# Moving a conversion piece's integer operations ahead of the weights' low parts in every odd slot of a retention, experts and feed-forward kernel

## The chip, the cores and the metric

The kernel runs on one core of a Trainium2 chip. The metric is the time of one execution in device microseconds; three runs of the kernel before took 1249.22, 1249.59 and 1250.06 us, with a median of 1249.59 us.

## The reference

Three stages follow each other, all in float32. First a retention layer (2 x 8 heads, 768 positions, 64 columns), whose output has 1536 rows of 512 columns. Then a layer of 8 experts, whose gate is normalised by eight rounds of row and column sums. Then a feed-forward layer with `h - tanh(h)`.

```python
def _moe_ref(x, w_gate, w1, w2):
    ...
    for _ in range(8):
        P /= P.sum(1, keepdims=True) + 1e-09
        P /= P.sum(0, keepdims=True) + 1e-09
        P *= N / E
    for e in range(E):
        h = np.maximum(x @ w1[e], 0.0)
        out += P[:, e:e + 1] * (h @ w2[e])

def _moe2_ref(x, w_in, w_out):
    h = x @ w_in
    return ((h - np.tanh(h)) @ w_out)
```

The weights of the last layer, `moe2_w_in` and `moe2_w_out`, arrive as 64-bit floats, two 32-bit words each, and the kernel itself turns them into float32.

## The kernel before

Every float32 operand of a product is split into a high part (`...h`, a copy rounded by ACT) and a low part (`...l`, the difference, made by DVE or POOL), and every product is three matmuls: high by high, low by high, high by low. `split` (L174) makes such a pair. Products of `x` and the first weights follow a Strassen scheme with seven products per block (`product`, L807; `xp...` are plain blocks of `x`, `xs...` sums of blocks).

The middle of the program is a loop over 64 **slots** (L835), each the work of one quarter of an expert's weights on one half of the rows. A slot has a fixed order on PE: products 1, 2, 5 and 6; the second matmuls (`tiles`, L617, result bank `yq`) of the slot before for its tiles 0 to 2; product 7; tiles 3 to 5; products 4 and 3. The banks of `yq` are three in turn, so tile 3 uses the bank of tile 0. DVE adds each `yq` to `yacc` (L641). Between the products ACT copies partial sums to SBUF (`sa`, `sb`) and DVE adds them to other banks (`pbl` L859, `pah` L871, `pbh` L882). ACT reads `sb` from the bank of `pal` before product 7 goes on adding to it. The hidden layer's high and low parts are `h0h`, `h0l`, `h1h`, `h1l` (`relu`, L677); DVE's second `h1l` of a slot frees the bank that the next slot's `pbh` writes.

Odd slots bring in the next weights. `w_load` (L117) loads them to `wraw`, which has one buffer; `w1_split` and `w2_split` make `w1h`, `w1l`, `w2h`, `w2l`. DVE makes two low parts of `w1l`, POOL the other four and those of `w2l`. The new `wraw` can be loaded when POOL has made the last `w2l`.

Beside this, from slot 5 to slot 60, the last layer's weights are converted in 64 **pieces** (`conv`, L563), one in most slots and two in ten even slots. A piece has steps: step 0 issues the load of the words `d` on SP's queue; step 1 is five integer operations on DVE (L580 to L587, on buffers `c0` and `c1`), then two on POOL (L588, L589); step 2 is two more on DVE (L591, L592), which wait for POOL; steps 3 to 5 split the result, or sums of results, into blocks `hl` (`block`, L553; five buffers in turn) and store them to DRAM (`wscr`). A store is not issued where its block is made: it is put on a list, and `flush` (L540) issues what stands there. At a step 1 all of the list is issued; at other steps only what came from earlier slots.

What is done at which point of a slot stands in four lists, `fd`, `fa`, `fb` and `fc`, filled from L733 on by `put` and emptied once in each slot: `fd` behind product 5, `fa` behind product 7, `fb` behind tile 5, `fc` at the slot's end. Each engine runs its instructions in the order in which they are written, and SP issues its DMAs in that order.

```python
flush(j == 1)
...
box[q, p].append(cq.tile([128, NC64], I32, tag=f"c1_{count[0] % 7}", name=f"c1_{u}_{i}"))
...
for steps in (((fa, s - 1), (fa, s), (fc, s)), ((fd, s), (fb, s), (fd, s + 1)))[:1 + more]:
```

The last line gives the places of steps 0, 1 and 2 of a slot's first and second piece.

Of the kernel before, what the change touches and what calls it, by code (L numbers as in the profile page):

```python
# [11 lines left out]
I32 = mybir.dt.int32  # L12
# [9 lines left out]
NCH = N // CH  # L22
# [14 lines left out]
NS = len(SLOTS)  # L37
NC64 = 256
# [17 lines left out]
def kernel(  # L56
# [27 lines left out]
    def bank(name):  # L84
        return psh.tile([128, 512], F32, tag="h", name=name)
# [118 lines left out]
    attn = ctx.enter_context(ExitStack())  # L204
# [331 lines left out]
    box = {}  # L536

    stores, now, count = [], [0], [0, 0, 0]

    def flush(all=False):  # L540
        while stores and (all or stores[0][0] < now[0]):
            stores.pop(0)[2]()
# [10 lines left out]
    def block(q, o, src, pair=False):  # L553
        tag = f"hl{count[1] % 5}"
        t = staged(tag, 256, f"hl{q}_{o}")
        count[1] += 1
        if pair:
            split(halves(t[:, 0]), halves(t[:, 1]), odds(src), nc.gpsimd)
        else:
            split(t[:, 0], t[:, 1], src, nc.gpsimd)  # L560
        store(q, o, t, tag)

    def conv(u, i, j):  # L563
        q, p = 2 * u + i // 8, i % 8
        flush(j == 1)
        if j == 0:
            d = cq.tile([128, NC64, 2], I32, tag=f"d{count[2] % 3}", name=f"d{u}_{i}")
            count[2] += 1
            nc.sync.dma_start(out=d.rearrange("p n t -> p (n t)"),
                              in_=wio[u].bitcast(I32)[:, i * 2 * NC64:(i + 1) * 2 * NC64])  # L570
            c0 = cp.tile([128, NC64], I32, tag="c0", name=f"c0_{u}_{i}")
            box[q, p] = [d, c0]
            return
        if j == 1:
            box[q, p].append(cq.tile([128, NC64], I32, tag=f"c1_{count[0] % 7}", name=f"c1_{u}_{i}"))
            count[0] += 1
        d, c0, c1 = box[q, p]
        hi, lo, val = d[:, :, 1], d[:, :, 0], c1.bitcast(F32)
        if j == 1:
            nc.vector.tensor_scalar(out=c0, in0=hi, scalar1=3, scalar2=0x40000000,  # L580
                                    op0=ALU.logical_shift_left, op1=ALU.bitwise_xor)
            nc.vector.tensor_scalar(out=c1, in0=hi, scalar1=-0x80000000, scalar2=None, op0=ALU.bitwise_and)
            nc.vector.scalar_tensor_tensor(out=c0, in0=c0, scalar=0x7FFFFFFF, in1=c1,
                                           op0=ALU.bitwise_and, op1=ALU.bitwise_or)
            nc.vector.tensor_scalar(out=val, in0=lo.bitcast(U32), scalar1=2.0 ** -52,
                                    scalar2=None, op0=ALU.mult)
            nc.vector.tensor_scalar(out=lo, in0=c0, scalar1=-0x800000, scalar2=None, op0=ALU.bitwise_and)  # L587
            nc.gpsimd.tensor_tensor(out=val, in0=val, in1=lo.bitcast(F32), op=ALU.mult)  # L588
            nc.gpsimd.tensor_tensor(out=val, in0=val, in1=c0.bitcast(F32), op=ALU.add)  # L589
        elif j == 2:  # L590
            nc.vector.tensor_scalar(out=lo, in0=hi, scalar1=0x7FFFFFFF, scalar2=None, op0=ALU.bitwise_and)  # L591
            nc.vector.scalar_tensor_tensor(out=val, in0=lo.bitcast(F32), scalar=thr, in1=val,  # L592
                                           op0=ALU.is_ge, op1=ALU.mult)
        elif j == 3:
            if p < 3:
                block(q, (0, 256, 1536)[p], val)
            elif p == 3:
                a11, a22 = (box[q, k][2].bitcast(F32) for k in (0, 2))
                nc.gpsimd.tensor_tensor(out=a22, in0=val, in1=a22, op=ALU.add)
                nc.gpsimd.tensor_tensor(out=val, in0=a11, in1=val, op=ALU.subtract)  # L600
            else:
                block(q, 1792 + 256 * (p - 4), val, True)
        elif j == 4:
            a11, a12, a22 = (box[q, k][2].bitcast(F32) for k in range(3))
            block(q, WI[5], a22)
            block(q, WI[7], val)
            nc.gpsimd.tensor_tensor(out=a11, in0=a22, in1=a11, op=ALU.subtract)
            nc.gpsimd.tensor_tensor(out=a12, in0=a12, in1=a11, op=ALU.subtract)
        else:
            a11, a12 = (box[q, k][2].bitcast(F32) for k in range(2))  # L610
            block(q, WI[6], a11)
            block(q, WI[3], a12)
# [117 lines left out]
        if X2[n][1]:  # L730
            x2_sum(b, X2[n][1], eng)

    spots = [{s: [] for s in range(NS)} for _ in range(4)]  # L733
    fd, fa, fb, fc = spots

    def put(f, s, what, *a):
        f[s].append(lambda: what(*a))

    for q in range(2, NQE):
        s = 2 * q - 1  # L740
# [35 lines left out]
    put(fa, 1, stage, 0)  # L776
    put(fa, 1, sblocks, NCH - 2)
    put(fb, 1, w2_split, 1, 0)
    put(fb, 1, raws, NCH - 3)
    put(fb, 1, raws, NCH - 2)  # L780
    for what, a in ((sblocks, (NCH - 1,)), (w2_split, (1, 1)), (raws, (NCH - 1,))):
        put(fc, 1, what, *a)
    for j in range(1, NST):
        put((fa, fc)[(j - 1) % 2], 2 + (j - 1) // 2, stage, j)
    for c in range(NCH):
# [3 lines left out]
    n = 0  # L789
    for s in range(lo_, hi_):  # L790
        more = s % 2 == 0 and (s - lo_) // 2 * extra // ((hi_ - lo_) // 2) != ((s - lo_) // 2 + 1) * extra // ((hi_ - lo_) // 2)
        for steps in (((fa, s - 1), (fa, s), (fc, s)), ((fd, s), (fb, s), (fd, s + 1)))[:1 + more]:
            for j, (f, at_) in enumerate(steps):
                put(f, at_, conv, n // (nconv // NQ), n % (nconv // NQ), j)
            f, at_ = (fd, at_ + 1) if f is fc else (fb, at_)
            for j in (3, 4, 5) if n % 8 == 3 else (3,):
                put(f, at_ + j - 3, conv, n // (nconv // NQ), n % (nconv // NQ), j)
            n += 1
# [31 lines left out]
    def run(fs):  # L830
        for f in fs:
            f()

    pend = None
    for s in range(NS):  # L835
        if s == 1:
            yp_, sm = (ctx.enter_context(tc.tile_pool(name=n, bufs=1, reuse_waits="tile")) for n in ("yp", "sm"))
        now[0] = s
        if s == 2:
            attn.close()  # L840
            attn = ctx.enter_context(ExitStack())
            cp = attn.enter_context(tc.tile_pool(name="cp", bufs=2, side="right", reuse_waits="tile"))
            cq = attn.enter_context(tc.tile_pool(name="cq", bufs=1, side="right", reuse_waits="tile"))
        if s == NS - 2:
            flush(True)
# [13 lines left out]
        nc.vector.tensor_tensor(out=pbl, in0=pbl, in1=sa, op=ALU.add)  # L859
        product(pbh, s, 5, True)  # L860
        nc.scalar.activation(out=sa, in_=pbh, func=ACTF.Copy)
        run(fd[s])
        product(pal, s, 6, False)
        nc.scalar.activation(out=sb, in_=pal, func=ACTF.Copy)
# [94 lines left out]
    for g in range(ng):  # L959
        f = [bank(f"f{i}_{g}") for i in range(2)]  # L960
# [122 lines left out]
```

## Time and profile before

| what | value |
|---|---|
| median of three runs | 1249.59 us |
| the profiled execution's own time | 1250.11 us |
| its span, first to last instruction | 1248.3 us |
| PE busy | 1233.6 us, 99% |
| DVE busy | 995.8 us, 80% |
| ACT busy | 589.8 us, 47% |
| POOL busy | 536.9 us, 43% |
| granted clock of TensorE | 1.000 over the span |

The own time is the span and 1.8 us around it. Busy shares are averages over the whole program, which has three stages. Times in the views are counted from the start of the span. Matmuls overlap: a row of 512 columns lasts 0.38 us, but the next starts 0.22 us later.

### The profile page before, as it was taken

Reading aid. Unit: us, or ns where it says so; the run is one execution under the profiler, and the core shown is the slowest. Engines: PE = TensorE matmul, PEld = TensorE weight load, DVE = VectorE, ACT = ScalarE, POOL = GpSimd, SP = SyncE. Lnnn points to the kernel's source line nnn. Section 1 sums busy time; section 2 is a strip of 40 time slices with the busy share of each in tenths; the row PEclk is TensorE's granted clock in tenths of the full one; section 3 lists DMA queues with packets and bytes.
Section 4 is the critical chain, followed back from the end, with each engine's and each line's share of the span. In section 5 each row is a group of like instructions: output and inputs, shape, how many; then the busy total and the mean of one; then the engine's idle time right before and its main releaser. Section 6 shows DMA issues by size and latency. Waiting matters only on the chain. (4 is left out here: it accounts for less than half of the span.)

```text
span 1248.3 us, 20284 instructions
## 1 busy us (share of the span) xinstructions
PE 1233.6 (99%) x7450; PEld 1138.0 (91%) x7450; DVE 995.8 (80%) x1914; ACT 589.8 (47%) x1191; POOL 536.9 (43%) x696
## 2 busy tenths in 40 slices
PE   8999999999999999999999999999999999999998
PEld 6899999999999999999999999999999889999997
DVE  6978888877778787787787878778785788888987
ACT  4653333433333433333333443333333388888875
POOL 4853444644645555554554654554462022131000
PEclk9999999999999999999999999999999999999999
DMA  9311122322322332322232232222334266384571
GB/s 327 132 34 43 43 68 68 112 83 68 110 68 78 103 111 81 110 76 77 76 93 77 88 98 77 85 85 77 94 95 182 93 233 232 110 279 143 199 266 68
DMA packets 63635, 141.84 MB, mean 114 GB/s; under 512 B 6064, under 2 KB 33200, under 8 KB 63536
## 3 DMA queue, kind: packets, MB, share of 16 engines
q1 hardware_dynamic: 63104, 140.02, 33.7%
q8 instruction: 58, 0.95, 0.3%
q10 hardware_dynamic: 432, 0.53, 0.1%
q14 instruction: 41, 0.34, 0.1%
HBM read 114.32 MB, written 26.21 MB: 113 GB/s over the span
## 5 line engine op out<-in xcount | busy, mean ns | idle before, releaser
L641 DVE SCALAR_TENSOR_TENSOR yacc<-yq,prob,yacc 128x512 f32<-128x512 f32 x336 | 240.1, 745 | 105.5 <-PE yq L628 104.9
L178 POOL TENSOR_TENSOR hl<-c,hl 128x256 fp32r<-128x256 f32 x88 | 71.1, 819 | 190.7 <-ACT hl L176 190.7
L626 PE MATMUL yq<-w2h,h1h 128*128 128x512 f32 x384 | 146.3, 381 | 0.0
L628 PE MATMUL yq<-w2h,h1l 128*128 128x512 f32 x384 | 145.6, 379 | 0.0
L627 PE MATMUL yq<-w2l,h1h 128*128 128x512 f32 x384 | 145.6, 379 | 0.0
L626 PE MATMUL yq<-w2h,h0h 128*128 128x512 f32 x384 | 145.5, 379 | 0.0
L627 PE MATMUL yq<-w2l,h0h 128*128 128x512 f32 x384 | 145.5, 379 | 0.0
L628 PE MATMUL yq<-w2h,h0l 128*128 128x512 f32 x384 | 145.5, 379 | 0.0
L813 PE MATMUL pal<-xsh,w1h 128*128 128x384 f32 x384 | 125.6, 327 | 0.0
L815 PE MATMUL pal<-xsl,w1h 128*128 128x384 f32 x384 | 125.2, 326 | 0.0
L816 PE MATMUL pal<-xsh,w1l 128*128 128x384 f32 x384 | 125.2, 326 | 0.0
L679 ACT ACTIVATE h1h<-pah 128x384 fp32r<-128x384 f32 x64 | 31.4, 491 | 177.5 <-PE yq L627 171.9
L588 POOL TENSOR_TENSOR c<-c,d 128x256 f32<-128x256 f32 x64 | 47.5, 742 | 138.5 <-DVE d L587 134.1
L178 POOL TENSOR_TENSOR w1l<-wsum,w1h 128x256 fp32r<-128x256 f32 x124 | 91.1, 765 | 31.5 <-ACT w1h L176 31.5
L178 POOL TENSOR_TENSOR w2l<-wraw,w2h 128x512 fp32r<-128x512 f32 x64 | 83.8, 1330 | 6.4 <-ACT w2h L176 6.4
L679 ACT ACTIVATE h0h<-pbl 128x384 fp32r<-128x384 f32 x64 | 31.7, 496 | 110.4 <-PE yq L627 110.4
L628 PEld LDWEIGHTS yq<-w2h,h1l 128*128 128x128 f32 x384 | 72.6, 189 | 10.7 <-DVE h1l L680 0.4
L627 PEld LDWEIGHTS yq<-w2l,h0h 128*128 128x128 f32 x384 | 72.6, 189 | 10.3
L628 PEld LDWEIGHTS yq<-w2h,h0l 128*128 128x128 f32 x384 | 72.6, 189 | 10.3
L626 PEld LDWEIGHTS yq<-w2h,h0h 128*128 128x128 f32 x384 | 72.6, 189 | 10.3
L626 PEld LDWEIGHTS yq<-w2h,h1h 128*128 128x128 f32 x384 | 72.6, 189 | 7.6 <-DVE yacc L641 0.5
L627 PEld LDWEIGHTS yq<-w2l,h1h 128*128 128x128 f32 x384 | 72.6, 189 | 7.1 <-POOL w2l L178 0.3
(228 smaller groups left out, 3599.0 us busy)
## 6 DMA issues: line engine op xcount, KB each, us to landing
wraw<-in_w SPq DMA_DIRECT2D x64, 512.0 KB, 4.8
wscr<-hl SPq DMA_DIRECT2D x88, 256.0 KB, 2.6
d<-in_wio SPq DMA_DIRECT2D x64, 256.0 KB, 3.3
w1h<-wscr SPq DMA_DIRECT2D x18, 768.0 KB, 4.5
w1l<-wscr SPq DMA_DIRECT2D x18, 768.0 KB, 5.9
w2h<-wscr SPq DMA_DIRECT2D x18, 512.0 KB, 3.8
w2l<-wscr SPq DMA_DIRECT2D x18, 512.0 KB, 4.7
qk<-in_qkv SPq DMA_DIRECT2D x11, 512.0 KB, 8.6
```

Of the source, the lines that this page charges most:

```text
L178: eng.tensor_tensor(out=lo, in0=src, in1=hi.bitcast(F32), op=ALU.subtract)
L588: nc.gpsimd.tensor_tensor(out=val, in0=val, in1=lo.bitcast(F32), op=ALU.mult)
L626: nc.tensor.matmul(out=yp, lhsT=hi, rhs=pairs(w2h[q][:, i]), start=i == 1, stop=False)
L627: nc.tensor.matmul(out=yp, lhsT=hi, rhs=pairs(w2l[q][:, i]), start=False, stop=False)
L628: nc.tensor.matmul(out=yp, lhsT=lo, rhs=pairs(w2h[q][:, i]), start=False, stop=i == 0)
L641: nc.vector.scalar_tensor_tensor(out=y, in0=yp, scalar=prob[:, c, q // 4:q // 4 + 1], in1=y, op0=ALU.mult, op1=ALU.add)
L679: nc.scalar.activation(out=hi, in_=ps, func=ACTF.Relu)
L813: nc.tensor.matmul(out=ps, lhsT=w1h[q][:, ws], rhs=pairs(xh[:, k]), start=start and k == 0, stop=False, skip_group_check=True)
L815: nc.tensor.matmul(out=ps, lhsT=w1h[q][:, ws], rhs=pairs(xl[:, k]), start=False, stop=False, skip_group_check=True)
L816: nc.tensor.matmul(out=ps, lhsT=w1l[q][:, ws], rhs=pairs(xh[:, k]), start=False, stop=k == 1, skip_group_check=True)
```

## The change

In odd slots step 1 of a piece moves from `fa`, behind product 7, to a new list `fe`, which is emptied right ahead of `fd`. Step 1 is also where `flush` issues the whole list of stores. `c0` is now taken at step 1 and has one buffer instead of two, and `c1` has eight instead of seven. In the start of the loop the split of the rows of chunks 9, 10 and 11 (`raws`) moves from slot 1 to `fd` of slot 2, the last blocks of sums (`sblocks`) come earlier within slot 1, and the pools of the first stage are closed one slot later.

```diff
-            c0 = cp.tile([128, NC64], I32, tag="c0", name=f"c0_{u}_{i}")
-            box[q, p] = [d, c0]
+            box[q, p] = [d]
             return
         if j == 1:
-            box[q, p].append(cq.tile([128, NC64], I32, tag=f"c1_{count[0] % 7}", name=f"c1_{u}_{i}"))
+            box[q, p].append(cp.tile([128, NC64], I32, tag="c0", name=f"c0_{u}_{i}"))
+            box[q, p].append(cq.tile([128, NC64], I32, tag=f"c1_{count[0] % 8}", name=f"c1_{u}_{i}"))
...
-    put(fb, 1, raws, NCH - 3)
-    put(fb, 1, raws, NCH - 2)
-    for what, a in ((sblocks, (NCH - 1,)), (w2_split, (1, 1)), (raws, (NCH - 1,))):
-        put(fc, 1, what, *a)
+    put(fb, 1, sblocks, NCH - 1)
+    put(fc, 1, w2_split, 1, 1)
+    for c in range(NCH - 3, NCH):
+        put(fd, 2, raws, c)
...
-        for steps in (((fa, s - 1), (fa, s), (fc, s)), ((fd, s), (fb, s), (fd, s + 1)))[:1 + more]:
+        for steps in (((fa, s - 1), ((fa, fe)[s % 2], s), (fc, s)), ((fd, s), (fb, s), (fd, s + 1)))[:1 + more]:
...
-        if s == 2:
+        if s == 3:
...
-            cp = attn.enter_context(tc.tile_pool(name="cp", bufs=2, side="right", reuse_waits="tile"))
+            cp = attn.enter_context(tc.tile_pool(name="cp", bufs=1, side="right", reuse_waits="tile"))
...
         nc.scalar.activation(out=sa, in_=pbh, func=ACTF.Copy)
+        run(fe[s])
         run(fd[s])
```

DVE in slot 23, before, from the addition to `pbl` to the first use of `h0l` (the number in a name is the slot, the piece or the load):

```order
L859 TENSOR_TENSOR pbl23_4249<-pbl23_4249,sa_896 128x384
L178 TENSOR_TENSOR w1l12_4275<-wraw12_4102,w1h12_4274 128x512
L178 TENSOR_TENSOR w1l12_4275<-wraw12_4102,w1h12_4274 128x256
L591 TENSOR_SCALAR d1_3_4136<-d1_3_4136 128x256
L592 SCALAR_TENSOR_TENSOR c1_1_3_4221<-d1_3_4136,c1_1_3_4221 128x256
L641 SCALAR_TENSOR_TENSOR yacc0_1065<-yq22_0_4292,prob_76,yacc0_1065 128x512
L641 SCALAR_TENSOR_TENSOR yacc0_1065<-yq22_1_4300,prob_76,yacc0_1065 128x512
L641 SCALAR_TENSOR_TENSOR yacc0_1065<-yq22_2_4308,prob_76,yacc0_1065 128x512
L871 TENSOR_TENSOR pah23_4322<-pal23_4248,sa_896 128x384
L580 TENSOR_SCALAR c0_1_4_4194<-d1_4_4192 128x256
```

The same place in the change:

```order
L859 TENSOR_TENSOR pbl23_4248<-pbl23_4248,sa_896 128x384
L580 TENSOR_SCALAR c0_1_4_4273<-d1_4_4191 128x256
L582 TENSOR_SCALAR c1_1_4_4274<-d1_4_4191 128x256
L583 SCALAR_TENSOR_TENSOR c0_1_4_4273<-c0_1_4_4273,c1_1_4_4274 128x256
L585 TENSOR_SCALAR c1_1_4_4274<-d1_4_4191 128x256
L587 TENSOR_SCALAR d1_4_4191<-c0_1_4_4273 128x256
L178 TENSOR_TENSOR w1l12_4283<-wraw12_4100,w1h12_4282 128x512
L178 TENSOR_TENSOR w1l12_4283<-wraw12_4100,w1h12_4282 128x256
L591 TENSOR_SCALAR d1_3_4135<-d1_3_4135 128x256
L592 SCALAR_TENSOR_TENSOR c1_1_3_4220<-d1_3_4135,c1_1_3_4220 128x256
L641 SCALAR_TENSOR_TENSOR yacc0_1065<-yq22_0_4300,prob_76,yacc0_1065 128x512
```

The five integer operations stood behind `pah` and now stand between `pbl` and the low parts; L591 and L592 belong to the second piece of slot 22. On POOL the two operations L588 and L589 move with them, ahead of the slot's `hl` and `w1l` parts.

SP's queue around slots 11 and 12, before (`wraw7` is the load at the end of slot 11; `hl0_512` to `hl0_2048` are made in slot 11, the three after them in slot 12):

```order
L551 DMA wscr0_77<-hl0_512_2562 256x1x256
L551 DMA wscr0_77<-hl0_1024_2565 256x1x256
L551 DMA wscr0_77<-hl0_1792_2570 256x1x256
L569 DMA d0_7_2630<-in_wio 128x512
L121 DMA wraw7_2685<-in_w12 128x1024 x2
L551 DMA wscr0_77<-hl0_2048_2665 256x1x256
L551 DMA wscr0_77<-hl0_768_2717 256x1x256
L551 DMA wscr0_77<-hl0_1280_2720 256x1x256
L551 DMA wscr0_77<-hl0_2304_2723 256x1x256
```

The same place in the change:

```order
L569 DMA d0_7_2627<-in_wio 128x512
L121 DMA wraw7_2681<-in_w12 128x1024 x2
L551 DMA wscr0_77<-hl0_512_2570 256x1x256
L551 DMA wscr0_77<-hl0_1024_2573 256x1x256
L551 DMA wscr0_77<-hl0_1792_2578 256x1x256
L551 DMA wscr0_77<-hl0_2048_2661 256x1x256
L551 DMA wscr0_77<-hl0_768_2716 256x1x256
L551 DMA wscr0_77<-hl0_1280_2719 256x1x256
L551 DMA wscr0_77<-hl0_2304_2722 256x1x256
```

Three stores that stood ahead of the loads of `d` and `wraw` now stand behind them. The blocks take the five `hl` buffers in turn in the order in which they are made: `hl0_1280` has the buffer of `hl0_512`, and `hl0_2304` that of `hl0_1024`.

DVE at the end of slot 1, the piece of the difference (`-` before, `+` the change, rows without a sign in both):

```order
-L178 TENSOR_TENSOR xpl_1_97<-xr_803,xph_1_94 128x4x64
-L178 TENSOR_TENSOR xpl_1_97<-xr_847,xph_1_94 128x4x64
-L680 SCALAR_TENSOR_TENSOR h1l<-pah_1089,h1h 128x384
-L680 SCALAR_TENSOR_TENSOR h1l<-pal_1015,h1h 128x384
-L882 TENSOR_TENSOR pbh_1017<-pbh_1017,sb 128x384
 L178 TENSOR_TENSOR xsl_1_95<-xr_744,xsh_1_92 128x8x64
 L178 TENSOR_TENSOR xsl_1_95<-ts_1046,xsh_1_92 128x4x64
 L178 TENSOR_TENSOR xsl_1_96<-ts_1046,xsh_1_93 128x4x64
+L680 SCALAR_TENSOR_TENSOR h1l<-pah_1089,h1h 128x384
+L680 SCALAR_TENSOR_TENSOR h1l<-pal_1015,h1h 128x384
+L883 TENSOR_TENSOR pbh_1017<-pbh_1017,sb 128x384
+L680 SCALAR_TENSOR_TENSOR h0l<-pbh_1017,h0h 128x384
```

The two `xpl` parts of chunks 9 and 10 leave slot 1, and the three `xsl` parts stand ahead of the two `h1l` instead of behind them. In slot 2 the three `xpl` parts of chunks 9 to 11 follow the addition to `pbl`.

## Rows read from the trace of the kernel before

**Rows 1.** The page: busy time of each engine, and two of the costliest groups.
```profile
PE 1233.6 (99%) x7450; PEld 1138.0 (91%) x7450; DVE 995.8 (80%) x1914; ACT 589.8 (47%) x1191; POOL 536.9 (43%) x696
...
L641 DVE SCALAR_TENSOR_TENSOR yacc<-yq,prob,yacc 128x512 f32<-128x512 f32 x336 | 240.1, 745 | 105.5 <-PE yq L628 104.9
...
L588 POOL TENSOR_TENSOR c<-c,d 128x256 f32<-128x256 f32 x64 | 47.5, 742 | 138.5 <-DVE d L587 134.1
```

**Rows 2.** Waits: engine, line, who was waited for, us in total, times, longest.
```profile
PEld yq L626 <- DVE yacc L641: 0.5, 2, 0.3
```

**Rows 3.** Timeline of PE at the end of slot 11: start, us, engine, line, operation.
```profile
229.54 0.43 PE L813 MATMUL pbh<-xsh,w1h 128*128 128x384 f32 x1 [0.43 <-DVE h1l L680]
```

**Rows 4.** Timeline of PE early in slot 2.
```profile
80.86 0.43 PE L815 MATMUL pbh<-xsl,w1h 128*128 128x384 f32 x1 [0.25 <-DVE xsl L178]
```

**Rows 5.** Timeline of DVE in slot 23.
```profile
393.55 1.03 DVE L178 TENSOR_TENSOR w1l<-wraw,w1h 128x512 fp32r<-128x512 f32 x2 [1.16 <-ACT w1h L176]
394.50 0.91 DVE L591 TENSOR_SCALAR d<-d 128x256 int32<-128x256 int32 x1
395.51 0.49 DVE L592 SCALAR_TENSOR_TENSOR c<-d,c 128x256 f32<-128x256 f32 x1
395.92 2.03 DVE L641 SCALAR_TENSOR_TENSOR yacc<-yq,prob,yacc 128x512 f32<-128x512 f32 x3
```

**Rows 6.** Timeline of PE in slot 23, first product of tile 3.
```profile
397.00 0.38 PE L626 MATMUL yq<-w2h,h1h 128*128 128x512 f32 x1
```

**Rows 7.** Timeline of all engines in slot 55.
```profile
863.94 2.03 DVE L641 SCALAR_TENSOR_TENSOR yacc<-yq,prob,yacc 128x512 f32<-128x512 f32 x3
...
865.01 0.38 PE L626 MATMUL yq<-w2h,h1h 128*128 128x512 f32 x1
```

**Rows 8.** Timeline of all engines in slot 17.
```profile
306.92 0.33 DVE L591 TENSOR_SCALAR d<-d 128x256 int32<-128x256 int32 x1
...
307.76 2.06 DVE L641 SCALAR_TENSOR_TENSOR yacc<-yq,prob,yacc 128x512 f32<-128x512 f32 x3
...
309.43 0.38 PE L626 MATMUL yq<-w2h,h1h 128*128 128x512 f32 x1
```

**Rows 9.** Timeline of DVE in slot 16, first and next after one piece's integer operations.
```profile
295.58 0.32 DVE L580 TENSOR_SCALAR c<-d 128x256 int32<-128x256 int32 x1
...
297.22 0.54 DVE L680 SCALAR_TENSOR_TENSOR h0l<-pbl,h0h 128x384 fp32r<-128x384 f32 x1
```

**Rows 10.** Timeline of POOL in slot 11.
```profile
226.25 0.75 POOL L588 TENSOR_TENSOR c<-c,d 128x256 f32<-128x256 f32 x1 [0.64 <-DVE d L587]
...
227.76 2.56 POOL L178 TENSOR_TENSOR w2l<-wraw,w2h 128x512 fp32r<-128x512 f32 x2
```

**Rows 11.** Timeline of SP's queue, slots 11 and 12.
```profile
230.35 0.81 SPq L121 DMA_DIRECT2D wraw<-in_w  x2
231.26 4.73 SPq L551 DMA_DIRECT2D wscr<-hl  x4
```

**Rows 12.** DMA issues from 231.1 to 231.9 us: KB each, us to landing.
```profile
wraw<-in_w SPq DMA_DIRECT2D x1, 512.0 KB, 5.4
wscr<-hl SPq DMA_DIRECT2D x1, 256.0 KB, 5.6
```

**Rows 13.** Timeline of all engines in slot 12.
```profile
233.86 0.48 ACT L864 ACTIVATE sb<-pal 128x384 f32<-128x384 f32 x1
...
235.48 0.33 PE L813 MATMUL pal<-xsh,w1h 128*128 128x384 f32 x1
```

**Rows 14.** Timeline of all engines in slot 32.
```profile
522.59 0.43 SPq L569 DMA_DIRECT2D d<-in_wio  x1
...
524.24 1.15 ACT L176 ACTIVATE hl<-c 128x256 fp32r<-128x256 f32 x3
...
527.38 0.33 PE L813 MATMUL pal<-xsh,w1h 128*128 128x384 f32 x1
```

**Rows 15.** DMA issues from 522.5 to 523 us: KB each, us to landing.
```profile
d<-in_wio SPq DMA_DIRECT2D x1, 256.0 KB, 5.0
```

More of the change, by code (lines that the diff above doesn't have):

```diff
@@ L731, in x2_step @@
             x2_sum(b, X2[n][1], eng)
-    spots = [{s: [] for s in range(NS)} for _ in range(4)]
-    fd, fa, fb, fc = spots
+    spots = [{s: [] for s in range(NS)} for _ in range(5)]
+    fd, fa, fb, fc, fe = spots
     def put(f, s, what, *a):
```

## The prediction, made before the change was run

> **What bounds the kernel now.** The page comes first: PE is busy for 99% of the span and DVE for 80% [rows 1], so inside the slots the kernel is bound by TensorE, and an edit on DVE, POOL or the DMA queue counts only where PE is made to wait, or is spared a wait. The second view is the waits of PE, the third the timelines around them. They show three kinds of wait in the slots.
>
> The first is at the end of slot 11: DVE runs late, the low part that frees the bank of `pbh` comes late, and PE sits idle for 0.43 us; the product that follows lasts 0.43 instead of 0.33 us, so a wait costs some 0.1 us more than itself [rows 3]. The second is early in slot 2, 0.25 us for a low part of `xs` and again 0.1 us after it [rows 4]. The third is the one to watch: tile 3 of a slot writes the bank of tile 0, so it waits until DVE has added tile 0 to `yacc`. That wait ended the idle time of the weight loads twice, 0.5 us in all [rows 2].
>
> How near the others are is seen in slot 23. After `pbl` DVE waits 1.16 us for ACT's `w1h`, makes the two low parts, then L591 and L592 of a piece left over from the slot before, and only then reaches `yacc` [rows 5]. This first addition starts at 395.92, lasts 0.74 [rows 1], ends at 396.66, and tile 3 starts at 397.00 [rows 6]. The margin is 0.34 us; I allow 0.05 of it for the signal. Slot 55 has the same: 863.94 + 0.74 = 864.68 against 865.01 [rows 7]. Six odd slots are like this (23, 27, 33, 43, 49, 55); slots 11, 39 and 59 have no margin; slot 17 has 0.93 us (308.50 against 309.43) [rows 8]. These ten follow an even slot with two pieces. In the other odd slots DVE reaches `yacc` ahead of PE; they are left out.
>
> **Term 1, the gains.** In slot 11 the integer operations leave the part behind `pah`, which is where DVE fell behind, so the wait at its end goes: 0.43 + 0.10 = 0.53 us [rows 3]. In slot 2 the `xs` parts now come ahead of the two `h1l`, and the 0.25 + 0.10 go [rows 4]. The three `xpl` parts that move to slot 2 are read by its last product, and the idle time of DVE there covers them; without that cover they would delay `yacc` as below. Together -0.9 us; bounds -0.5 (the `h1l` behind the `xs` parts come later and eat the second) to -1.1.
>
> **Term 2, tile 3 waits for DVE.** Five integer operations now stand between `pbl` and the low parts. With POOL idle beside them they run from 295.58 to 297.22, 1.64 us [rows 9]. They fill the 1.16 us, less the overlap of 0.09 with which one instruction enters behind another, and what is left delays everything behind by 1.64 - 1.16 - 0.09 = 0.39, say 0.4 us.
>
> POOL's two operations on the piece now run ahead of its `hl` parts, right when DVE reaches L591 and L592. L591 took 0.91 us in slot 23 and 0.33 in slot 17 [rows 5, 8]; it is slow where POOL works beside it. In slot 23 that wait is paid already, but L592 fell into a pause of POOL (0.49). With POOL busy it is nearer to 0.8, 0.3 more. So yacc's first addition comes 0.7 us later in the six slots: 0.7 - 0.3 margin + 0.1 = 0.5 each, 3.0 us. In slots 11, 39 and 59 L592 is slow already: 0.4 each, 1.2 us. In slot 17 both are fast: 0.4 + 0.6 + 0.3 - 0.9 + 0.1 = 0.5 us. Sum +4.7 us. The bounds: if L592 stays fast, 6 x 0.2 + 1.2 + 0.2 = 2.6; if the integer operations themselves meet POOL in some of these slots, half a microsecond more each, some 7. I take 4.7, as L591 shows that POOL's work slows such an operation.
>
> One buffer for `c0` instead of two makes the next piece wait for POOL's L589 of the last. I cost this at nothing: where a slot has two pieces, DVE does three additions to `yacc` between them (2.03 us [rows 5]), longer than POOL's two operations of 0.74 [rows 1]. POOL's `w1l` come up to 1.5 us later, by the same two operations; they are for the next slot, and no wait of PE on them stands in the list: nothing either.
>
> **Term 3, the stores go behind the weight load.** In an odd slot the flush of stores now comes before that slot's parts are made, so SP issues them only in the next slot, behind `wraw`. That load waits for its buffer, until POOL's `w2l` is done: 227.76 + 2.56 = 230.32, issue at 230.35 [rows 10, 11]. What is issued behind it lands behind it: the second half, issued at 230.74, takes 5.4 us (236.1); the store issued at 231.26 takes 5.6 (236.8) [rows 11, 12]. In slot 32's case the load of `d` behind `wraw` is issued at 522.59 and lands 5.0 us later, at 527.6 [rows 14, 15].
>
> Five `hl` buffers go round. Where a slot makes three blocks and the next three more, a buffer is wanted again at once. Slot 12 is the worst: its second and third block reuse the buffers of the first two stores of slot 11, ACT writes them just ahead of `sb`, which starts at 233.86 [rows 13]. Product 7 adds to the bank that `sb` reads, and PE comes to it at 235.48 [rows 13]. In the change POOL's `w2l` ends some 0.7 us earlier (the pause of 0.64 before L588 [rows 10] is gone), so the first store takes the place of the one above at 236.8 - 0.7 = 236.1 and the second, the same size again, follows some 0.7 later, 236.8. Then the third `hl` (0.5) and `sb` (0.48) end at 237.8. PE is there at 235.48 - 0.53 + 0.4 = 235.3: a wait of 2.5, with 0.1 for the restart and 0.1 for the signals 2.7 us. In slots 32 and 52 only the third block reuses the first store of the slot before: 527.6 - 0.7 = 526.9, `hl` and `sb` 1.0, so 527.9 + 0.1 against 527.38 [rows 14]: 0.6 + 0.1 = 0.7 us, twice. Sum +4.1 us. Bounds: nothing, if the stores land early, to 6, if POOL's `w2l` gains nothing and slot 32's late `hl` makes POOL collide with DVE.
>
> **Sum.** -0.9 + 4.7 + 4.1 = +7.9 us. The profiled execution took 1250.11 us, 0.52 above the median of the runs shown, so it would become 1258.0, and the median 1249.59 + 7.9 = 1257.5 us.
>
> **Rivals.** A: *not slower*. The point that decides is L591: if POOL is quiet when DVE reaches it, it costs 0.33 as in slot 17 [rows 8], 0.58 less than in slot 23 [rows 5]; this outweighs the 0.4 of term 2, `yacc` comes no later, tile 3 never waits, and the two waits of rows 2 go as well. With stores that land in time that is 1249.59 - 0.9 - 0.5 = 1248.2 us. For it: 1.16 us of idle DVE time in every odd slot is real. Against it: POOL starts as soon as L587 ends, before L591. B: *the stores land alone*, some 3 us after their issue; then only terms 1 and 2 count: 1249.59 + 3.8 = 1253.4 us. Against it stand both landings in rows 12 and 15. C: *DVE holds its margins* and only terms 1 and 3 count: 1249.59 + 3.2 = 1252.8 us. D: *the second low part waits too*. POOL's L588 would start inside the first `w1l` part, stand first in line, and hold up the second by some 0.5 of its 0.74 us [rows 1], in ten slots: 1257.5 + 5 = 1262.5 us. Against it: the second part enters 0.09 us before the first is done (1.03 us for both, and L591 only then [rows 5]), so POOL finds no gap there.
>
> The Trainium skill, page "SBUF — State Buffer", section "SBUF: two separate sides", states the rule behind D: VectorE and GpSimd share one pair of ports as an exclusive lock, an operation with two SBUF inputs counts too, and whoever starts first holds it for the whole instruction. By the rule the time would be that of D, by the rows that of the forecast. The two durations of L591 agree with the lock as such.
>
> **How the numbers follow.** Chances: forecast 0.44, A 0.15, B 0.18, C 0.15, D 0.08. A measurement of this kernel can tell about 0.2%, 2.5 us, from no change: below 1247.1 is faster, above 1252.1 slower. A lies within, a fifth of its spread below; B lies above, with a tenth of its spread within; C lies above, with a third of its spread (low bounds of term 3) within. That makes 0.03 faster, 0.12 + 0.02 + 0.05, some 0.2, the same, and 0.77 slower. The range leaves out A and half of D, and goes down to C with its lower bounds, some 2 us below its centre: 1250.5 to 1262.0 us.
>
> **What would show it.** Right: PE's waits list `yq` L626 on DVE `yacc` some ten times, and product 7's `pal` L813 on ACT `sb` in slots 12, 32 and 52, with ACT's `hl` waiting for a store. Integer operations fill DVE's pause before `w1l`. Wrong: no wait of PE on `sb` (term 3), `yacc` as early as before (term 2), or the wait at the end of slot 11 still there (term 1).

## The result, and the profile after

The changed kernel took 1265.45 us (median of four runs, 1265.09 to 1265.85) against 1249.82 us for the kernel before (1249.22 to 1251.09). The ratio is 1.0123, with a 95% interval of 1.0111 to 1.0135: 15.6 us slower. The prediction said slower, but by 7.9 us, and its range ended at 1262.0. The profiled execution took 1265.85 us, 15.74 more than that of before.

The page of the changed kernel, busy time of the engines and two groups:

```profile
PE 1238.7 (98%) x7450; PEld 1140.2 (90%) x7450; DVE 1004.1 (79%) x1914; ACT 586.2 (46%) x1191; POOL 534.8 (42%) x696
...
L626 PE MATMUL yq<-w2h,h1h 128*128 128x512 f32 x384 | 147.2, 383 | 8.2 <-DVE yacc L641 8.2
...
L813 PE MATMUL pal<-xsh,w1h 128*128 128x384 f32 x384 | 125.9, 328 | 3.5 <-ACT sb L865 3.5
```

The number of instructions is the same as before [rows 1]; what is new is the idle time. The waits of PE name two sources that the list of before hardly had (engine, line, who was waited for, us in total, times, longest):

```profile
PE yq L626 <- DVE yacc L641: 8.2, 10, 1.5
PE pal L813 <- ACT sb L865: 3.5, 3, 1.3
...
PE pbh L813 <- DVE h1l L680: 0.9, 3, 0.4
```

Ten waits of tile 3 and three of product 7: these are the places that terms 2 and 3 had named. The list counts idle time only. Measured from start to start of the matmuls, the 64 slots became 14.1 us longer in the profiled execution: 10.45 in the ten tile-3 waits with their slower restarts (what three of them lost before taken off), 4.27 in the three waits on `sb`, 0.36 at the end of slot 32, less 0.69 at the end of slot 11 and 0.45 in slot 2; the rest is 0.24 at tile 3 of slot 7, less 0.1 of small ones. Some 0.7 us each came ahead of the slots and behind them, and 0.3 outside the span. Ahead of them TensorE's clock is the likely cause: at 13 us PE is 2.0 us behind the execution of before, and waits that became shorter took back all but 0.7. The windows of the first microseconds (busy time of each engine, then granted clock, DMA share, GB/s) have a stretch at half speed, the lower of the two levels, that the execution of before did not have:

```profile
5.00:10.00 5.00, 3.27 (x33) 2.71 (x32) 3.67 (x9) 0.00 (x0) 0.44 (x1) 0.82 1.00 366
10.00:15.00 5.00, 4.42 (x48) 4.00 (x48) 4.10 (x9) 0.60 (x1) 1.74 (x2) 0.50 1.03 390
```

Nothing that the change touches runs there. The 0.7 us behind the slots stand behind the last matmul: the last two stores of the output land 2.9 and 2.8 us after their issue, where they took 2.2 and 2.1.

**Tile 3 in slot 23.** The timeline of DVE in the changed kernel, from the addition to `pbl` on; it answers to [rows 5]:

```profile
395.77 0.56 DVE L859 TENSOR_TENSOR pbl<-pbl,sa 128x384 f32<-128x384 f32 x1
396.23 0.31 DVE L580 TENSOR_SCALAR c<-d 128x256 int32<-128x256 int32 x1
...
397.67 0.34 DVE L587 TENSOR_SCALAR d<-c 128x256 int32<-128x256 int32 x1
397.89 1.56 DVE L178 TENSOR_TENSOR w1l<-wraw,w1h 128x512 fp32r<-128x512 f32 x2
399.37 0.89 DVE L591 TENSOR_SCALAR d<-d 128x256 int32<-128x256 int32 x1
400.30 0.88 DVE L592 SCALAR_TENSOR_TENSOR c<-d,c 128x256 f32<-128x256 f32 x1
401.06 1.43 DVE L641 SCALAR_TENSOR_TENSOR yacc<-yq,prob,yacc 128x512 f32<-128x512 f32 x2
```

POOL and PE beside it:

```profile
398.09 1.08 POOL L588 TENSOR_TENSOR c<-c,d 128x256 f32<-128x256 f32 x1 [3.46 <-DVE d L587]
399.25 0.80 POOL L589 TENSOR_TENSOR c<-c,c 128x256 f32<-128x256 f32 x1
400.01 0.84 POOL L178 TENSOR_TENSOR hl<-c,hl 128x256 fp32r<-128x256 f32 x1
...
401.89 0.48 PE L626 MATMUL yq<-w2h,h1h 128*128 128x512 f32 x1 [0.70 <-DVE yacc L641]
```

From the start of `pbl` to the first `yacc` it was 4.07 us before (391.85 to 395.92) and is 5.29 now, 1.22 more. Read from start to start: the low parts begin 0.42 later, the pair takes 0.53 longer (1.56 against 1.03), L591 is 0.08 shorter, L592 is 0.35 longer. The pair's growth is the one that the forecast had left out: the first part still takes 0.68 us, the second 0.97 instead of 0.42. L588 starts 0.20 us after the first part does.

**Product 7 in slot 12.** The timeline of ACT, and PE's first matmul of product 7, which answers to [rows 13]:

```profile
232.79 0.41 ACT L176 ACTIVATE hl<-c 128x256 fp32r<-128x256 f32 x1
236.93 0.42 ACT L176 ACTIVATE hl<-c 128x256 fp32r<-128x256 f32 x1 [3.72 <-DMA wscr<-hl]
237.54 0.44 ACT L176 ACTIVATE hl<-c 128x256 fp32r<-128x256 f32 x1 [0.20 <-DMA wscr<-hl]
237.88 0.47 ACT L865 ACTIVATE sb<-pal 128x384 f32<-128x384 f32 x1
...
238.41 0.43 PE L813 MATMUL pal<-xsh,w1h 128*128 128x384 f32 x1 [1.34 <-ACT sb L865]
```

ACT stands 3.72 us ahead of the second block because the store of slot 11 has not left its buffer, `sb` stands behind, and PE waits 1.34 us.

### The profile page after: what moved, and what is told of

Its sections match the earlier page's. It is cut to its first block, busy times and chain, and to the rows that moved or that the text cites. A ratio compares the mean times of both kernels' runs of the same rounds, so it can differ in the third digit from the quotient of the medians.

```text
span 1263.8 us, 20288 instructions
## 1 busy us (share of the span) xinstructions
PE 1238.7 (98%) x7450; PEld 1140.2 (90%) x7450; DVE 1004.1 (79%) x1914; ACT 586.2 (46%) x1191; POOL 534.8 (42%) x696
## 5 line engine op out<-in xcount | busy, mean ns | idle before, releaser
L641 DVE SCALAR_TENSOR_TENSOR yacc<-yq,prob,yacc 128x512 f32<-128x512 f32 x336 | 243.3, 746 | 129.9 <-PE yq L628 129.2
L588 POOL TENSOR_TENSOR c<-c,d 128x256 f32<-128x256 f32 x64 | 56.1, 877 | 246.1 <-DVE d L587 246.1
L178 POOL TENSOR_TENSOR hl<-c,hl 128x256 fp32r<-128x256 f32 x88 | 65.4, 752 | 122.8 <-ACT hl L176 122.8
L178 POOL TENSOR_TENSOR w1l<-wsum,w1h 128x256 fp32r<-128x256 f32 x124 | 88.7, 745 | 18.9 <-ACT w1h L176 18.9
L178 POOL TENSOR_TENSOR w2l<-wraw,w2h 128x512 fp32r<-128x512 f32 x64 | 82.7, 1312 | 6.3 <-ACT w2h L176 6.3
L628 PEld LDWEIGHTS yq<-w2h,h1l 128*128 128x128 f32 x384 | 72.6, 189 | 10.7 <-DVE h1l L680 0.4
L813 PEld LDWEIGHTS pal<-xsh,w1h 128*128 128x128 f32 x384 | 72.6, 189 | 8.3 <-ACT sb L865 4.7
```

What stands on the lines that cost most here:

```text
L178: eng.tensor_tensor(out=lo, in0=src, in1=hi.bitcast(F32), op=ALU.subtract)
L628: nc.tensor.matmul(out=yp, lhsT=lo, rhs=pairs(w2h[q][:, i]), start=False, stop=i == 0)
L641: nc.vector.scalar_tensor_tensor(out=y, in0=yp, scalar=prob[:, c, q // 4:q // 4 + 1], in1=y, op0=ALU.mult, op1=ALU.add)
L813: nc.tensor.matmul(out=ps, lhsT=w1h[q][:, ws], rhs=pairs(xh[:, k]), start=start and k == 0, stop=False, skip_group_check=True)
```

## The experiments

All times are medians; "before" is the kernel before, run beside them on the same chip (1249.76 to 1250.30 us in the four groups of runs, so a difference between runs of two groups is uncertain by some half a microsecond). Ratios are to it.

### 1 to 3: POOL's two operations, and the stores

The first edit leaves POOL's L588 and L589 behind product 7 (`pool_part` is these two):

```diff
-            nc.gpsimd.tensor_tensor(out=val, in0=val, in1=lo.bitcast(F32), op=ALU.mult)
-            nc.gpsimd.tensor_tensor(out=val, in0=val, in1=c0.bitcast(F32), op=ALU.add)
+            if at == 0:
+                pool_part(u, i)
...
+                if f is fe:
+                    put(fa, at_, conv, n // (nconv // NQ), n % (nconv // NQ), j, 2)
```

The second issues the stores of odd slots where they were issued before; the third makes both edits.

```diff
-        flush(j == 1)
+        flush(j == 1 and now[0] % 2 == 0)
...
+            if s % 2:
+                put(fa, s, flush, True)
```

> The changed kernel, but POOL's two operations of a piece's step 1 (L588, L589) stay where they were before the change, behind product 7 (list fa); DVE's five integer operations stay early (fe). Theory (contention): of the 1.21 us by which yacc comes later in slot 23 of the changed kernel, 0.41 is the integer operations themselves, 0.53 the second w1l part beside L588 and 0.35 L592 beside POOL. Without the two POOL operations the tile-3 waits, 10.9 us in all with their restarts, fall to between 3 and 7 us (POOL's hl part now meets DVE 0.4 us later in DVE's list than before the change, so some contention comes back). POOL's w2l ends about 0.7 us later, so the stores behind wraw cost up to 2 us more. Time 1258 to 1263 us. Rival (length of DVE's list): DVE is late by its own work, whoever runs beside it; the waits stay near 0.9 us each and the time at 1264 to 1267 us.

> The changed kernel, but in odd slots the list of stores is emptied at the old place (end of fa), not at the early step 1. Theory (stores behind wraw): the three waits of product 7 on ACT's sb, 1.5 + 1.24 + 1.22 us and 0.1 us of restart each in slots 12, 32 and 52, go, and nothing else changes: 1265.45 - 4.3 = 1261.2 us. Rival (ACT's hl comes late because POOL and DVE are late with the piece): the waits stay, 1264 to 1266 us.

> Both edits together. Theory (contention, and stores behind wraw, independent of each other): no wait on sb, tile-3 waits of 3 to 7 us, so 1253 to 1257 us, by the same amounts as the two runs alone give. Rival (the stores are late as a result of late DVE and POOL work): the second edit adds nothing to the first, 1258 us and above.

Measured: 1262.32 us (ratio 1.0095, 1.0082 to 1.0109), 1258.97 us (1.0069, 1.0055 to 1.0083) and 1254.78 us (1.0036, 1.0022 to 1.0049). PE's waits in the second and the third run (of the third also those of the weight loads, PEld, which stand ahead of the matmuls and show the short waits too):

```profile
PE yq L626 <- DVE yacc L641: 8.2, 10, 1.5
PE o L331 <- POOL qd L285: 1.7, 2, 1.2
```

```profile
PE yq L635 <- DVE yacc L650: 3.6, 6, 0.9
...
PEld yq L635 <- DVE yacc L650: 6.9, 10, 1.2
```

With the stores at their old place no wait on `sb` is left, and the slots are 5.1 us shorter in the profiled execution: the three waits with their restarts, 4.27, the late end of slot 32, which was behind the same late block, and little else. The median fell by 6.5, 2.2 more than expected and 1.4 more than the slots show; the two profiled executions also differ by 0.65 us ahead of the slots, where the clock was at 1.00 in that of run 2, and by 0.7 behind them. The first edit took 4.2 us off the ten waits. Together the edits gave 10.7 us, alone 3.1 and 6.5. The first gives less by itself: PE comes to product 7 of slot 12 earlier then, waits 2.0 us for `sb` instead of 1.3, and loses more behind that wait, since its clock falls (last section).

But the third run still waits ten times with POOL's two operations gone, and its DVE shows why (slot 23; `w1l` is L178, L594 and L595 are the old L591 and L592):

```profile
394.73 1.55 DVE L178 TENSOR_TENSOR w1l<-wraw,w1h 128x512 fp32r<-128x512 f32 x2
396.20 0.33 DVE L594 TENSOR_SCALAR d<-d 128x256 int32<-128x256 int32 x1
396.57 0.85 DVE L595 SCALAR_TENSOR_TENSOR c<-d,c 128x256 f32<-128x256 f32 x1
```

```profile
394.96 1.04 POOL L178 TENSOR_TENSOR hl<-c,hl 128x256 fp32r<-128x256 f32 x1 [3.48 <-ACT hl L176]
396.28 3.12 POOL L178 TENSOR_TENSOR w1l<-wsum,w1h 128x256 fp32r<-128x256 f32 x4 [0.28 <-ACT w1h L176]
```

POOL's `hl` part, which stood there before the change too, has taken the place of L588: it starts 0.23 us after the first `w1l` part, and the pair again takes 1.55. In the kernel before it started 0.66 us after the first part (393.55 [rows 5]) and the pair took 1.03:

```profile
394.21 0.97 POOL L178 TENSOR_TENSOR hl<-c,hl 128x256 fp32r<-128x256 f32 x1 [3.59 <-ACT hl L176]
```

L591's successor, which starts while POOL is idle, is at 0.33. So a delay of DVE by 0.4 us is enough to bring the two engines together.

### 4: the part of slot 2 alone

```diff
-    put(fb, 1, raws, NCH - 3)
-    put(fb, 1, raws, NCH - 2)
...
+    for c in range(NCH - 3, NCH):
+        put(fd, 2, raws, c)
```

> The kernel before with the start of the loop alone taken from the change (xpl parts of chunks 9 to 11 in slot 2, pools closed one slot later). Theory: PE's lost time at the start of slot 2 falls from 0.74 to 0.29 us as in the changed kernel: 1249.82 - 0.45 = 1249.4 us, within the spread of the runs. Rival (this part costs something elsewhere, in the yacc of slot 2): above 1250.5 us.

Measured: 1249.33 us, ratio 0.9994 (0.9985 to 1.0003). In the trace slot 2 loses 0.33 us instead of 0.74. The size is as expected, too small for the runs to tell from nothing.

### 5, 6 and 9: how many of the five fit

In run 5 three of the five operations go ahead of the low parts, in run 6 four; the others, POOL's two and the flush stay behind product 7 (`integers` runs a range of the five; at 6 also POOL's two). The edit is that of run 5; run 6 has 4 in the place of 3:

```diff
+                k = (0, 3)[s % 2] if f is fe else 6
+                put(f, at_, conv, n // (nconv // NQ), n % (nconv // NQ), j, *([k] if f is fe else []))
+                if f is fe:
+                    if k < 6:
+                        put(fa, s, integers, n // (nconv // NQ), n % (nconv // NQ), k, 6)
+                    put(fa, s, flush, True)
```

> The changed kernel, but in odd slots only the first three integer operations (L580, L582, L583) go ahead of the low parts; the other two, POOL's two and the flush of all stores stay behind product 7. Theory (the pause has room for about 1.16 us, and what stays inside it moves nothing): the three take 1.03 us in the changed kernel's slot 23, so the low parts start when they did before the change, no tile-3 wait is added, and DVE has 1 us less behind product 7: the wait at the end of slot 11 (0.69 us with its restart) goes, on top of the part of slot 2: 1249.33 - 0.7 = 1248.6 us. Rival (any operation ahead of the low parts costs): 1250 us or more.

> As the run with three operations, but with four ahead of the low parts (1.41 us in slot 23 of the changed kernel). Theory (a cliff: a little past the pause the second w1l part meets POOL's hl part, whose start waits for ACT alone): w1l starts some 0.3 us later, its second part takes 0.96 instead of 0.42 us, and the ten slots wait nearly as with five operations in the third run, some 5.5 us in all: 1253 to 1254.5 us. Rival (the cost grows with the operations' own length alone): 0.3 us later against margins of 0.3, waits only in slots 11, 39 and 59, 1249 to 1250 us.

Measured: 1248.07 us (0.9987, 0.9978 to 0.9995) with three and 1248.58 us (0.999, 0.9981 to 0.9999) with four. Three behaves as expected. Slot 23 of that run, DVE and then POOL:

```profile
391.33 0.42 DVE L612 SCALAR_TENSOR_TENSOR c<-c,c 128x256 int32<-128x256 int32 x1
391.98 1.03 DVE L178 TENSOR_TENSOR w1l<-wraw,w1h 128x512 fp32r<-128x512 f32 x2 [0.22 <-ACT w1h L176]
...
392.63 0.97 POOL L178 TENSOR_TENSOR hl<-c,hl 128x256 fp32r<-128x256 f32 x1 [3.48 <-ACT hl L176]
```

A pause of 0.22 us is left and the low parts start when they did. With four, neither the cliff nor its rival came: no tile-3 wait at all. I had put the low parts 0.3 us later; they are only 0.09 later (1.79 from `pbl`, 1.70 before), since at both ends of the pause an instruction overlaps its neighbour by some 0.1. But in other slots of the same run the edge is to be seen. The timelines of DVE and POOL in slot 19 and then in slot 23:

```profile
331.99 1.56 DVE L178 TENSOR_TENSOR w1l<-wraw,w1h 128x512 fp32r<-128x512 f32 x2
...
332.55 2.31 POOL L178 TENSOR_TENSOR hl<-c,hl 128x256 fp32r<-128x256 f32 x3 [6.01 <-ACT hl L176]
...
391.24 1.01 DVE L178 TENSOR_TENSOR w1l<-wraw,w1h 128x512 fp32r<-128x512 f32 x2
...
391.82 1.02 POOL L178 TENSOR_TENSOR hl<-c,hl 128x256 fp32r<-128x256 f32 x1 [3.50 <-ACT hl L176]
```

In slot 23 POOL starts 0.58 us after the pair and the pair takes 1.01 us; in slot 19 it starts 0.56 us after, and the pair takes 1.56. Over the 27 odd slots of this run from 7 to 59, seven had POOL start 0.123 to 0.128 us ahead of the first part's end and a second part of 0.96 or 0.97 us; in 19 POOL started 0.104 or less ahead of it, behind it or not at all, and the second part took 0.40 to 0.42. Slot 7 does not fit: POOL started 0.138 ahead there, and the second part took 0.43:

```profile
158.67 1.03 DVE L178 TENSOR_TENSOR w1l<-wraw,w1h 128x512 fp32r<-128x512 f32 x2
...
159.22 1.07 POOL L178 TENSOR_TENSOR hl<-c,hl 128x256 fp32r<-128x256 f32 x1 [6.45 <-ACT hl L176]
```

Why is open; the expectation of run 9 below states the edge without this slot. The seven cost nothing, since DVE reaches `yacc` ahead of PE in those slots.

If this is the edge, a little more work on DVE must push the ten slots over it. The ninth run repeats a quarter of L585 behind the fourth operation, in the 27 odd slots with a piece:

```diff
+        if hi_op == 4:
+            nc.vector.tensor_scalar(out=val[:, 0:64], in0=lo.bitcast(U32)[:, 0:64], scalar1=2.0 ** -52,
+                                    scalar2=None, op0=ALU.mult)
```

> The run with four early operations, and one short repeat behind them: a quarter of L585's columns once more, some 0.15 to 0.2 us on DVE, with the same result. In the four-operation run the second w1l part took 0.96 us where POOL's hl part had started 0.123 us or more before the first part ended, and 0.42 where 0.104 or less. Theory (who starts first): the repeat moves the first w1l part past that edge in the slots that were short of it, the second part takes 0.96 us there, L592 meets POOL as in the third run; the ten slots wait 0.3 to 1.0 us each, 4 to 6 us in all: 1252.5 to 1254.5 us, for 64 x 0.2 us of work on an engine that is idle a fifth of the time. Rival (DVE's own length): 0.2 us against a margin of 0.1 to 0.2, at most 0.2 in each of ten slots: 1248.6 to 1250.5 us.

Measured: 1253.70 us (1.0027, 1.0016 to 1.0038), 5.1 us above the run with four (4.6 when each is counted from the kernel before on its own chip). Slot 23, DVE and POOL:

```profile
393.83 0.21 DVE L620 TENSOR_SCALAR c<-d 128x64 f32<-128x64 uint32 x1
393.96 1.56 DVE L178 TENSOR_TENSOR w1l<-wraw,w1h 128x512 fp32r<-128x512 f32 x2
...
394.30 0.93 POOL L178 TENSOR_TENSOR hl<-c,hl 128x256 fp32r<-128x256 f32 x1 [3.49 <-ACT hl L176]
```

An instruction of 0.21 us makes the pair 0.55 us longer, and PE's waits of tile 3 come back:

```profile
PE yq L638 <- DVE yacc L653: 3.0, 6, 0.8
```

### 10: all five, with POOL kept away

As the third run, and the low parts of `hl` of the same place wait until product 7 as well:

```diff
+        if defer[0]:
+            split(*args, (0,))
+            late.append(lambda: split(*args, (1,)))
```

> The third run (five early operations, POOL's two late, stores early), and POOL's low parts of the blocks hl that it makes in the same place of odd slots also go behind product 7, so that POOL has nothing to do beside DVE's w1l and L591. Theory (contention, not DVE's own length): the second w1l part is back at 0.42 us and L591 at 0.33; only L592 may meet POOL's w1l. yacc comes 0.41 - 0.58 + 0.35 = 0.2 us later than before the change, inside the margin of six slots; in slots 11, 39 and 59 up to 0.3 and in 17 some 0.2 remain. 1250 us or less, some 4.5 us under the third run. Rival (five operations are too long by themselves, 0.41 us past the pause): the waits of the third run stay, 1253.5 us or more.

Measured: 1249.31 us (0.9991, 0.9981 to 1.0), 5.5 us under the third run with the same work on every engine. Slot 23, DVE, and POOL's next instruction:

```profile
393.38 1.01 DVE L178 TENSOR_TENSOR w1l<-wraw,w1h 128x512 fp32r<-128x512 f32 x2
394.30 0.34 DVE L589 TENSOR_SCALAR d<-d 128x256 int32<-128x256 int32 x1
394.68 0.53 DVE L590 SCALAR_TENSOR_TENSOR c<-d,c 128x256 f32<-128x256 f32 x1
395.09 2.09 DVE L657 SCALAR_TENSOR_TENSOR yacc<-yq,prob,yacc 128x512 f32<-128x512 f32 x3
...
394.95 2.19 POOL L178 TENSOR_TENSOR w1l<-wsum,w1h 128x256 fp32r<-128x256 f32 x3 [4.79 <-ACT w1h L176]
```

Five operations ahead of the low parts, and the first `yacc` comes 3.83 us after the start of `pbl`, 0.24 sooner than before the change. One tile-3 wait is left, in slot 17, where POOL's `w1l` still meets L591 and L592. This is rival A's mechanism, made to work by moving POOL.

### 11 and 12: which stores, and the stores alone

The eleventh run gives only slots 11, 31 and 51 the old place of the flush; the twelfth is the kernel before with the early flush alone, in odd slots, in the place of the old one:

```diff
-        flush(j == 1)
+        flush(j == 1 and now[0] not in (11, 31, 51))
```

```diff
-        flush(j == 1)
+        flush(j == 1 and now[0] % 2 == 0)
...
+        if s % 2 and lo_ <= s < hi_:
+            flush(True)
         run(fd[s])
```

> The changed kernel, with the stores issued at the old place (end of fa) in slots 11, 31 and 51 alone, and late in the other odd slots. Theory (a store behind wraw costs only where its hl buffer is wanted again at once): the whole gain of the second run comes back, 1258.97 us within half a microsecond, and PE does not wait on sb. Rival (the stores crowd the queue everywhere): less than half of that gain, 1262 us or more.

> The kernel before, with one thing of the change alone: in odd slots the list of stores is emptied ahead of fd instead of behind product 7, so that the slot's own stores stand behind the next wraw. Theory: product 7 waits for sb in slots 12, 32 and 52 as in the changed kernel, 1.2 to 2.2 us each (POOL's w2l ends later here than in the changed kernel, which may make them longer, as in the first run), and slot 32's end is later: +4 to +6.5 us, 1254 to 1256.5 us. Rival (the waits on sb in the changed kernel come from its late DVE and POOL work): no wait on sb, 1249 to 1251 us.

Measured: 1259.70 us (1.0078, 1.0062 to 1.0095) and 1262.83 us (1.0101, 1.0086 to 1.0116). The first is 0.7 us above the second run, a little more than I allowed, but no wait on `sb` is left in its list and its slots are as long in all (958.6 against 958.8 us from their first matmul to their last): three stores' places hold the whole of term 3. The last shows the term alone, and larger than I expected:

```profile
PE pal L813 <- ACT sb L866: 7.2, 3, 3.2
```

```profile
237.62 0.42 ACT L176 ACTIVATE hl<-c 128x256 fp32r<-128x256 f32 x1 [4.07 <-DMA wscr<-hl]
```

The block in slot 12 waits 4.07 us for its store and PE 3.21 for `sb`, where it was 1.34 in the changed kernel. Two things make the difference of 1.87, counted from the start of slot 11 in both. POOL's last `w2l`, on which the load of `wraw` and the stores behind it wait, ends 1.25 us later here (18.34 against 17.09), since POOL waits 0.62 us for L587 and makes L588 and L589 right ahead of it; and PE comes to product 7 0.65 sooner, as no tile-3 wait has held it up. In slots 32 and 52 PE comes at the same time in both kernels, and the wait is longer by the later `w2l` alone (1.0 us of 2.1 in slot 32). So the change shortened term 3 by what it did to POOL. The waits with their restarts are 8.0 of the 9.8 us by which the slots grew in the profiled execution (1260.85 us, the lowest of the four runs); the clock, below, is 1.7 more. The other three runs have no profile; their granted clocks of 0.996 and 0.997, against 0.998 in this one, point to more of the same.

### 7 and 8: the even slots

Even slots have no low parts of `w1` on DVE, and their first `yacc` comes 2.6 us ahead of tile 3. The seventh run moves the whole step 1 there instead of in the odd slots; the eighth has this and the three operations of the fifth run. The edit is that of the eighth; the seventh has `(fe, fa)` and `(6, 0)` in the places of `(fe, fe)` and `(6, 3)`.

```diff
-        for steps in (((fa, s - 1), ((fa, fe)[s % 2], s), (fc, s)), ((fd, s), (fb, s), (fd, s + 1)))[:1 + more]:
+        for steps in (((fa, s - 1), ((fe, fe)[s % 2], s), (fc, s)), ((fd, s), (fb, s), (fd, s + 1)))[:1 + more]:
...
+                k = (6, 3)[s % 2] if f is fe else 6
```

> The conversion's whole step 1 goes early in the even slots instead of the odd ones, with the flush of all stores where it was and the part of slot 2 kept. Even slots have no low parts of w1 on DVE, DVE is idle for 1.5 us in slot 32 at that place and its first yacc is 2.6 us ahead of tile 3. Theory: no tile-3 wait; the waits at the ends of slots 32, 38 and 58 (0.23, 0.39 and 0.37 us, and 0.1 each to restart) go, because the integer operations no longer stand behind product 7, and with them the small waits in slots 39 and 59: 1249.33 - 1.6 = 1247.7 us. Rival (POOL's two operations now push its hl and wsum work to where DVE works, and what is won is given back): 1249.3 us or more.

> Three early operations in odd slots and the whole step 1 early in even slots. Theory: both gains add, 1249.33 - 0.7 - 1.6 = 1247.0 us, faster than the kernel before by 0.2%. Rival: as for the even slots alone, no better than 1248.6 us.

Measured: 1247.10 us (0.9978, 0.9969 to 0.9987) and 1246.01 us (0.997, 0.9959 to 0.9982). Both are better than expected, by 0.6 and 1.0 us, and the eighth is faster than the kernel before by 0.3% and than the changed one by 19.4 us. PE's list of waits names no place in the slots any more; all its rows are of the first and the last stage, these first:

```profile
PE o L331 <- POOL qd L285: 1.7, 2, 1.2
PE warm L244 <- DVE zr L240: 1.5, 1, 1.5
```

## Why the prediction was wrong

**What bounds the kernel** was right: PE's own work did not change, and the slots grew by 14.1 us, nearly all of it waits at the places that were named.

**Term 1, -0.9 us**, came out at -1.14: the wait at the end of slot 11 went (0.69 with its restart, where 0.53 was booked) and slot 2 lost 0.29 instead of 0.74. Not foreseen was 0.36 at the end of slot 32, behind that slot's late block.

**Term 2, +4.7 us, is the step that failed: it was 10.45 us.** The forecast put five operations at 0.4 us past the pause, and slot 23 shows 0.42. It put L592 at 0.3 more beside POOL, and it was 0.35 later. What it priced at nothing was the second `w1l` part, 0.53 us in each of nine slots and more in slot 11, where L588 and the first part started at the same moment (218.60) and both parts were slowed: the pair took 2.17 us against 1.03. This is rival D, which had a chance of 0.08. It was set aside with the sentence that the second part enters 0.09 us before the first is done, so that POOL finds no gap. That holds where POOL starts when the first part is nearly done, as in the slot of [rows 5] (0.04 us ahead of its end). The changed kernel has POOL start 0.2 us after it, and then POOL is first in line: runs 6 and 9 put the edge at some 0.1 us ahead of the first part's end. Run 10, with the same work and POOL moved away, has the 0.42 back. In slot 17 both L591 and L592 were slowed as forecast, and 0.53 came on top: 0.99 us against 0.5. In slots 11, 39 and 59 it was 3.5 us together against 1.2. Two smaller readings were off: slot 33 was counted among the six with 0.34 us to spare and had 0.16, and slot 7, left out as one where DVE is early, waited 0.24.

The rule named beside rival D (the Trainium skill, page "SBUF — State Buffer", section "SBUF: two separate sides": whoever starts first holds the shared ports for the whole instruction) agrees with the traces of runs 3, 5, 6, 9 and 10: the second part takes 0.42 or 0.96 us by POOL's start, in every odd slot from 7 to 59 but slot 7 of run 6. Close to the edge who starts first does not settle it: POOL's start 0.046 us ahead of the second part's own slowed it in slot 19 of run 6, and 0.014 us ahead in slot 23 did not.

**Term 3, +4.1 us**, came out at 4.27, and 4.63 with the end of slot 32. The sum was right and its parts were not: 1.6 us in slot 12 instead of 2.7, since PE was already late by the tile-3 wait of slot 11, which the sum had put at 0.4 us; 1.3 in slots 32 and 52 each instead of 0.7, since the store landed 6.1 us after its issue, where the 5.0 of the load of `d` [rows 15] was taken. In run 12, where POOL's `w2l` ends later, the same waits are 8.0 us, so the earlier `w2l` that the sum had booked was real (0.7 us booked, 0.9 to 1.0 against the kernel before); the three places are the only ones that matter (run 11).

**The rivals.** A, B and C fall with the waits that were seen. D was the case, and its own 1262.5 us was still 3 us short: the larger waits of slot 11, 17, 39 and 59, and 0.7 us each ahead of the slots and behind them.

## What to carry to other kernels

The length of an idle stretch on one engine does not say what fits into it: ask what stands behind it and which instruction of another engine would then start first. Here three operations in a pause of 1.16 us, and four as well, made the slots 1.2 us shorter on top of the part of slot 2, and an instruction of 0.21 us more lost some 5. Moving a step also moves whatever is tied to it, here a flush of the store list; price each queue by itself and look for the next buffer that is wanted, and look first for a place where the margin is long (2.6 us in the even slots).

## What the runs showed of the hardware that was not expected

The edge is narrow: where POOL started 0.56 us after the pair of low parts the pair took 1.56 us, where it started 0.58 us after it 1.01, with the one exception of run 6. In the changed kernel DVE's additions from PSUM to `yacc` took 0.73 to 0.75 us without POOL beside them and 0.73 to 0.78 with it, while operations on SBUF alone went from 0.33 to 0.89 (L591), 0.49 to 0.88 (L592) and 0.42 to 0.97 (second `w1l`). POOL pays too: L588 took 1.08 us in slot 23 against 0.75 in [rows 10].

After a wait the clock of TensorE can fall to its lower level, 1.2 of 2.4 GHz. In the first run PE waited 2.0 us for `sb` in slot 12, and the windows around it (busy time of PE, PEld, DVE, ACT and POOL, then granted clock, DMA share, GB/s) show it:

```profile
236.00:238.00 2.00, 0.25 (x1) 0.25 (x2) 0.56 (x1) 1.53 (x4) 1.24 (x2) 1.00 0.90 317
238.00:240.00 2.00, 2.00 (x8) 1.91 (x8) 0.28 (x1) 0.08 (x1) 2.00 (x4) 0.56 0.74 249
240.00:242.00 2.00, 2.00 (x7) 1.59 (x6) 1.93 (x5) 0.00 (x0) 0.98 (x2) 0.59 0.96 297
```

In the twelfth run it fell after a wait of 2.1 us in slot 32, at a cost of 1.7 us, and not after the 3.2 us in slot 12 (granted clock 1.00 in all the windows behind it). So the length of the wait alone did not decide, and a wait of some 2 us can cost nearly its own length again. What decides is left open.
